# Weights of a feed-forward block loaded and decoded in 256-row chunks, with the masks built ahead of the branch

## The chip, the cores and the metric

The kernel runs on one core of a Trainium2 chip. The metric is the device time in microseconds (us); lower is better. TensorE (PE) multiplies matrices, VectorE (DVE) and ScalarE (ACT) work elementwise, GpSimd (POOL) fills small tiles, and SyncE (SP) issues the DMAs.

## What is computed

Three blocks stand one behind the other. The change touches what the first two need: the masks of the attention, and the weights `w_in` and `w_out` of the second block.

```python
# 1: banded attention, batch 2, 8 heads, 768 positions, head size 64
scores = q @ k.T / sqrt(64)
keep   = (pos_k < n_sink) | ((0 <= pos_q - pos_k) & (pos_q - pos_k < window))
a      = softmax(where(keep, scores, -1e9));   x = a @ v          # x: 2 x 768 x 512
# 2: gated feed-forward block
h      = relu(x @ w_in)                                           # w_in: 512 x 1024
gate   = sigmoid(conv3(h, conv_w));   x = (h * gate) @ w_out      # w_out: 1024 x 512
# 3: rotation by angles x @ w_theta, two token mixes (768 x 768), channel mix
z      = x * cos(x @ w_theta), x * sin(x @ w_theta)
u      = x + w_tok_r @ z_r + w_tok_i @ z_i;   out = u + relu(u @ w_ch)
```

`n_sink` (4) and `window` (128) are inputs, known only at run time. The weights arrive as 64-bit floats.

## The kernel before

**Order of the program.** `params` reads `n_sink` and `window` and works out a flag: do they allow the banded path, with at most two key blocks for a query block? Each engine loads that flag (`values_load`) and branches into `body`, in the banded form here. The instructions of `body` are put in order by a scheduler at build time; each engine then goes through its own list strictly in that order. SP too: a DMA whose tile isn't free yet holds up all DMAs behind it.

**Attention.** A *unit* is half the sequence of one batch element, four units in all. A unit has four pairs of heads, and each head has three *score tiles* of 128 queries (line 286 for the matmul, 288 for mask and maximum on DVE, 292 for the exponential on ACT). So there are 24 tiles in a unit and 96 in all; I count them as tile 1 to tile 96. The first tile of a batch element's first unit is 128 keys wide, others 260. Numbers 25 to 48 belong to the second unit. Behind the exponential comes the normalised probability, split in two halves, and its transpose: through PE for the first four heads (`transposed_by_pe`), through a DMA transpose (`pt<-pb`, line 322) for the others. `values` (line 190) makes the values ready for each pair of heads in the first unit of a batch element: load of `vt`, sum on ACT (203), scaled copy on ACT (209), subtraction on DVE (210), DMA transpose (`vp<-slot`, 212).

**Weights.** `weight_load` brings 128 rows by 512 columns of 64-bit words (512 KB) into a slot; `decode_parts` rebuilds 32-bit floats with one ACT operation (98) and three DVE operations (99, 100, 101), and `split` makes a high and a low part (80 on ACT, 82 on DVE): four DVE and two ACT operations of 512 elements for each of 16 chunks. The order is: four chunks for the first half of `w_in`, four for `w_out`, then the same again. The table `CHUNKS` says how many chunks are taken after which pair of heads of which unit. `BLOCKS` does the same for the feed-forward blocks (`Group.blocks`), whose matmuls are `ps_h` (122 to 124) and `ps_x` (616 to 622).

**Slots.** Weights and values share six slots of 4 KB on each partition, handed out in turn (`Slots`). A value takes two slots, one for the loaded rows, one for its two halves; a slot is free once its last reader is done.

**Ahead of the branch** stand the loads of chunk 0 and chunk 1, of the first queries and keys and of `conv_w`, the first three DVE steps of chunk 0 and the decoding of `conv_w`. The masks (`banded_masks`, lines 175 to 184) are built behind the branch.

Of the kernel before, what the change touches and what calls it, by code (L numbers as in the profile page):

```python
# [31 lines left out]
CHUNKS = ((1, 1, 3, 6), (2, 2, 0, 1), (0, 0, 0, 0), (0, 0, 0, 0))  # L32
# [4 lines left out]
DEC = 2  # L37
# [91 lines left out]
def params(tc, c, n_sink, window):  # L129

    nc = tc.nc
    raw = c.const.tile([P, 4], I32, name="par_raw")
    nc.sync.dma_start(raw[:, 0:2], n_sink.bitcast(I32).partition_broadcast(P))
    nc.sync.dma_start(raw[:, 2:4], window.bitcast(I32).partition_broadcast(P))
# [32 lines left out]
def banded_masks(tc, c):  # L167
# [3 lines left out]
    m, slot = c.raw.tile([P, 5 * P + 2 * NS], F32)  # L171
    m0, m1, m2 = m[:, :P], m[:, P : 3 * P + NS], m[:, 3 * P + NS :]
# [17 lines left out]
def values(tc, c, b, p):  # L190
# [533 lines left out]
def body(tc, c, general):  # L724
# [224 lines left out]
```

## Time and profile before

| what | us |
|---|---|
| median of 3 runs (461.37 to 462.35) | 461.46 |
| the profiled execution's own time | 463.23 |
| its span from first to last instruction | 461.4 |
| PE busy in the span | 413.2 |
| DVE busy in the span | 334.2 |
| ACT busy in the span | 291.5 |
| tile 1 starts on DVE | 14.87 |
| tile 48 (the second unit's last) starts on DVE | 108.31 |

Times in rows count from the start of the span. In a row of the timeline stand start, duration, engine, line, operation and, in brackets, how long the engine sat idle before it and what released it. In a row of the windows view stand, for each engine, busy time and number of instructions.

### The profile page before, as it was taken

Reading aid. Unit: us, or ns where it says so; the run is one execution under the profiler, and the core shown is the slowest. Engines: PE = TensorE matmul, PEld = TensorE weight load, DVE = VectorE, ACT = ScalarE, POOL = GpSimd, SP = SyncE. Lnnn points to the kernel's source line nnn. Section 1 sums busy time; section 2 is a strip of 40 time slices with the busy share of each in tenths; the row PEclk is TensorE's granted clock in tenths of the full one; section 3 lists DMA queues with packets and bytes.
Section 4 is the critical chain, followed back from the end, with each engine's and each line's share of the span. In section 5 each row is a group of like instructions: output and inputs, shape, how many; then the busy total and the mean of one; then the engine's idle time right before and its main releaser. Section 6 shows DMA issues by size and latency. Waiting matters only on the chain.

```text
span 461.4 us, 7204 instructions
## 1 busy us (share of the span) xinstructions
PE 413.2 (90%) x2376; PEld 334.9 (73%) x2376; DVE 334.2 (72%) x898; ACT 291.5 (63%) x717; POOL 35.5 (8%) x120
## 2 busy tenths in 40 slices
PE   1587739699889999999999999899979999999995
PEld 0465528587677887988888887688858888888874
DVE  3879989999889886865699877995599963211132
ACT  2799878978899886875685778875675431100010
POOL 4001210031221110110000000000000000000000
PEclk9989867899999999999999999999999999999999
DMA  6786999459888442212435200230037620000012
GB/s 180 208 230 148 248 247 293 107 117 201 181 169 166 103 92 48 47 38 39 139 88 164 70 1 0 70 92 23 0 93 223 195 84 23 24 23 24 23 45 75
DMA packets 73245, 50.07 MB, mean 109 GB/s; under 512 B 59376, under 2 KB 62448, under 8 KB 73200
## 3 DMA queue, kind: packets, MB, share of 16 engines
q1 hardware_dynamic: 73200, 49.54, 42.6%
q8 instruction: 20, 0.33, 0.3%
q14 instruction: 25, 0.20, 0.1%
HBM read 32.09 MB, written 3.15 MB: 76 GB/s over the span
## 4 chain that ended last, share of the span: by engine, by line
PE 67%; DVE 16%; DMA 8%; ACT 4%; issue 3%; SPq 1%; POOL 0%; DVEq 0%; ACTq 0%; POOLq 0%
PE ps_y L123 7%; PE ps_y L124 7%; PE ps_y L122 7%; PE ps_x L616 5%; PE ps_s L272 5%; PE ps_x L617 4%; PE ps_m L122 4%; PE ps_x L622 4%; PE ps_m L124 4%; PE ps_m L123 4%; PE ps_o L380 4%; PE ps_h L122 4%; PE ps_h L124 3%; PE ps_h L123 3%; DMA pt<-pb 3%
## 5 line engine op out<-in xcount | busy, mean ns | idle before, releaser
L272 PE MATMUL ps_s<-qk 128*128 128x260 f32 (+1 forms) x192 | 60.4, 420 | 20.4 <-DVE mx L288 11.1
L122 PE MATMUL ps_y<-z_hi,wt_hi 128*128 128x512 f32 x144 | 57.7, 401 | 1.6 <-ACT z_hi L80 1.6
L122 PE MATMUL ps_h<-xg_hi,win_hi 128*128 128x258 f32 x192 | 58.6, 307 | 0.4 <-ACT h L597 0.4
L124 PE MATMUL ps_y<-z_lo,wt_hi 128*128 128x512 f32 x144 | 56.7, 397 | 0.4 <-DVE z_lo L82 0.4
L123 PE MATMUL ps_y<-z_hi,wt_lo 128*128 128x512 f32 x144 | 56.9, 395 | 0.0
L124 PE MATMUL ps_h<-xg_lo,win_hi 128*128 128x258 f32 x192 | 56.0, 296 | 0.4 <-DVE xg_lo L401 0.3
L272 PEld LDWEIGHTS ps_s<-qk 128*128 128x128 f32 x192 | 34.2, 211 | 29.5 <-DVE mx L288 15.6
L123 PE MATMUL ps_h<-xg_hi,win_lo 128*128 128x258 f32 x192 | 55.4, 290 | 0.0
L80 ACT ACTIVATE xt_hi<-ps_t 128x512 fp32r<-128x512 f32 x24 | 14.0, 594 | 61.1 <-PE ps_t L650 61.0
L292 ACT ACTIVATE e<-e,mx 128x260 f32<-128x260 f32 (+1 forms) x96 | 47.3, 496 | 7.2 <-DVE mx L288 6.9
L601 DVE SCALAR_TENSOR_TENSOR cv<-h,cw_t,cv 128x256 f32<-128x256 f32 x96 | 44.8, 478 | 6.8 <-ACT cv L599 6.1
L288 DVE CUSTOM_DVE_ANT_0 e<-ps_s,m 128x260 f32<-128x260 f32 (+1 forms) x96 | 37.7, 399 | 10.4 <-PE ps_s L272 9.0
L616 PE MATMUL ps_x<-wout_hi,ghi 128*128 128x512 f32 x96 | 40.9, 426 | 3.4 <-ACT ghi L80 3.4
L718 DVE SCALAR_TENSOR_TENSOR slot<-ps_m,slot 128x512 f32<-128x512 f32 x12 | 8.3, 691 | 44.1 <-PE ps_m L124 44.1
L122 PEld LDWEIGHTS ps_h<-xg_hi,win_hi 128*128 128x128 f32 x192 | 36.8, 192 | 3.7 <-ACT h L597 1.2
L617 PE MATMUL ps_x<-wout_lo,ghi 128*128 128x512 f32 x96 | 38.7, 403 | 0.0
L124 PEld LDWEIGHTS ps_h<-xg_lo,win_hi 128*128 128x128 f32 x192 | 36.8, 193 | 1.9 <-issue 0.5
L123 PEld LDWEIGHTS ps_h<-xg_hi,win_lo 128*128 128x128 f32 x192 | 36.9, 192 | 1.4
L314 ACT ACTIVATE pb<-e,ri 128x256 f16<-128x256 f32 (+1 forms) x84 | 35.4, 494 | 1.9 <-DVE ri L296 1.2
L315 DVE SCALAR_TENSOR_TENSOR pb<-e,ri,pb 128x256 f16<-128x256 f32 (+1 forms) x84 | 35.5, 459 | 1.2 <-ACT pb L314 1.1
L380 PE MATMUL ps_o<-pt,vp 128*64 128x256 f16 (+2 forms) x348 | 23.8, 261 | 11.8 <-DMA pt<-pb 5.4
L380 PEld LDWEIGHTS <-vp 128*64 128x64 f16 (+1 forms) x348 | 17.9, 113 | 22.5 <-issue 13.3
(134 smaller groups left out, 927.6 us busy)
## 6 DMA issues: line engine op xcount, KB each, us to landing
raw<-in_w_tok_r_dram SPq DMA_DIRECT2D x12, 384.0 KB, 3.3
raw<-in_w_tok_i_dram SPq DMA_DIRECT2D x12, 384.0 KB, 3.5
slot<-in_w_in_dram SPq DMA_DIRECT2D x8, 512.0 KB, 6.1
slot<-in_w_out_dram SPq DMA_DIRECT2D x8, 512.0 KB, 4.7
qk<-in_q_dram SPq DMA_DIRECT2D x32, 96.0 KB, 3.3
slot<-in_vt_dram SPq DMA_DIRECT2D x8, 384.0 KB, 3.7
out_dram<-slot SPq DMA_DIRECT2D x12, 256.0 KB, 2.0
qk<-in_k_dram SPq DMA_DIRECT2D x8, 262.0 KB, 3.2
```

The lines of the kernel that those rows point to most:

```text
L122: nc.tensor.matmul(out, whi, xhi, start=first, stop=False)
L123: nc.tensor.matmul(out, wlo, xhi, start=False, stop=False)
L124: nc.tensor.matmul(out, whi, xlo, start=False, stop=last)
L272: nc.tensor.matmul(ps[:, :n], qk[0][:, a, i * P : (i + 1) * P], qk[1][:, o : o + n], start=True, stop=True)
L288: nc.vector.tensor_tensor_reduce(out=e[:, i, :n], in0=ps[:, :n], in1=m, scale=-1.0 / math.sqrt(D), scalar=3.0e38, op0=ALU.add, op1=ALU.min ...
L292: nc.scalar.activation(e[:, i, :n], e[:, i, :n], AF.Exp, bias=mx[:, i : i + 1], scale=-1.0, accum_out=sm[:, i : i + 1])
L314: nc.scalar.activation(hi, src, AF.Copy, scale=r)
L315: nc.vector.scalar_tensor_tensor(lo, src, r, hi, ALU.mult, ALU.subtract)
L380: nc.tensor.matmul(po[a * D : (a + 1) * D, q], w[:, a * D : (a + 1) * D], pts[a][: w.shape[0], b0:b1, :], start=(n == 0), stop=(n == len(j ...
L601: nc.vector.scalar_tensor_tensor(cv[:, n, :], h[:, n, k : GT + k], w[:, k : k + 1], cv[:, n, :], ALU.mult, ALU.add)
L616: nc.tensor.matmul(self.px[t], ghi[:, n, s], whi, start=f2 == 0 and n == 0, stop=False)
L617: nc.tensor.matmul(self.px[t], ghi[:, n, s], wlo, start=False, stop=False)
```

## The change

`params`: `window` is loaded through ACT's DMA queue, `n_sink` through SP's, and the flag comes after six DVE operations instead of ten. `banded_masks` is called ahead of the branch. The three decoding steps of chunk 0 and the decoding of `conv_w` are taken behind the branch. A weight chunk is 256 rows (1 MB), decoded in operations of 1024 elements: 8 chunks instead of 16, with `CHUNKS` rewritten. There are three slots of 8 KB instead of six of 4 KB. A value takes one slot: loaded rows in one half, its parts in the other. There is one buffer for `dec_t` (`DEC`) instead of two, of twice the size.

```diff
-CHUNKS = ((1, 1, 3, 6), (2, 2, 0, 1), (0, 0, 0, 0), (0, 0, 0, 0))
+CHUNKS = ((1, 0, 1, 3), (1, 1, 0, 1), (0, 0, 0, 0), (0, 0, 0, 0))
-DEC = 2
+DEC = 1
-EARLY = 1
@@ class Slots
-        self.free = [pool.tile([P, 2 * DM], I32, name=f"slot{i}") for i in range(n)]
+        self.free = [pool.tile([P, 4 * DM], I32, name=f"slot{i}") for i in range(n)]
@@ params
+    nc.scalar.dma_start(raw[:, 2:4], window.bitcast(I32).partition_broadcast(P))
     nc.sync.dma_start(raw[:, 0:2], n_sink.bitcast(I32).partition_broadcast(P))
-    nc.sync.dma_start(raw[:, 2:4], window.bitcast(I32).partition_broadcast(P))
...
-    nc.vector.tensor_copy(flag, t[:, 0:1])
+    nc.vector.scalar_tensor_tensor(flag, c.ns, float(NS), t[:, 1:2], ALU.is_le, ALU.mult)
+    w = c.const.tile([P, 2], F32, name="par_w")
+    nc.vector.scalar_tensor_tensor(w, flag.to_broadcast([P, 2]), 0.0, v, ALU.mult, ALU.add)
@@ values
-    raw, slot0 = c.raw.tile([P, S], F32)
+    both, slot = c.raw.pair(F32)
+    raw, parts = both[:, :S], both[:, S : 2 * S].bitcast(F16).rearrange("p (a k) -> p a k", a=2)
     nc.sync.dma_start(raw, c.vt[b, p * P : (p + 1) * P, :])
-    parts, slot1 = c.raw.tile([P, 2, S], F16)
@@ weight_load
-    n, i = divmod(i, 8)
-    if i < CC:
-        src = c.w_in[i * P : (i + 1) * P, 2 * n * DM : 2 * (n + 1) * DM]
+    n, i = divmod(i, 4)
+    if i < 2:
+        src = c.w_in[2 * i * P : 2 * (i + 1) * P, 2 * n * DM : 2 * (n + 1) * DM]
...
-    raw, slot = c.raw.tile([P, DM, 2], I32)
+    raw, slot = c.raw.pair()
@@ moe_weights
-        for tiles in (w1, w2):
-            for r in range(4):
...
+        for hi, lo in w1 + w2:
+            raw, slot = c.wraw.pop(0) if c.wraw else weight_load(tc, c, c.nw)
+            decode_parts(nc, c.dec, raw, hi, lo, INPLACE)
@@ body
-    if not general:
-        banded_masks(tc, c)
...
+        if n == 1:
+            conv_weights(tc, c)
@@ moe_stack
-        c.raw = Slots(c.const, B * NG)
+        c.raw = Slots(c.const, B * NG // 2)
...
-        with tc.tile_pool(name="dec0", bufs=1, side="right") as dec:
-            c.first = decode(nc, raw, dec.tile([P, DM], F32, name="dec_t"), True), slot
+        cw = conv_load(tc, c)
+        banded_masks(tc, c)
```

The engines' lists show where things stand now. First DVE, around the branch (`TENSOR_LOAD` and `COMPARE_AND_BRANCH`). Before:

```order
L150 CAST par_flag<-par_t 128x1
L99 TENSOR_SCALAR slot_100<-slot_100 128x512
L100 SCALAR_TENSOR_TENSOR slot_100<-dec_t,slot_100 128x512
L101 SCALAR_TENSOR_TENSOR slot_100<-slot_100 128x512
L99 TENSOR_SCALAR cw<-cw 128x24
L100 SCALAR_TENSOR_TENSOR cw_t<-cw_t,cw 128x24
L101 SCALAR_TENSOR_TENSOR cw_t<-cw,cw_t 128x24
L883 TENSOR_LOAD par_flag
L886 COMPARE_AND_BRANCH
L175 TENSOR_SCALAR slot_102<-rel 128x128
```

The same place now (the rows end with the first score tile and the first decoding step of the weights):

```order
L188 SCALAR_TENSOR_TENSOR slot_99<-col,par_w,slot_99 128x128
L191 TENSOR_SCALAR m_96<-slot_99 128x260
L191 TENSOR_SCALAR m_94<-slot_99 128x128
L191 TENSOR_SCALAR m_95<-slot_99 128x260
L888 TENSOR_LOAD par_flag
L892 COMPARE_AND_BRANCH
L295 ISA e,mx<-ps_s,m_94 128x128
L295 ISA mx 128x1
L106 TENSOR_SCALAR slot_98<-slot_98 128x1024
L106 TENSOR_SCALAR cw<-cw 128x24
```

The masks `m` moved ahead of the branch, and the decoding moved behind it, in between the score tiles.

Second SP, where the last two values of the first batch element and the first `w_out` chunks are brought in. Before, with six slots (numbers 100 to 105):

```order
L212 DMA_TRANSPOSE vp<-slot_104 128x12x128
L198 DMA slot_103<-in_vt_dram 128x768
L261 DMA qk_194<-in_q_dram 64x384
L212 DMA_TRANSPOSE vp<-slot_102 128x12x128
L551 DMA slot_105<-in_w_in_dram 128x1024
L261 DMA qk_194<-in_q_dram 64x384
L551 DMA slot_102<-in_w_out_dram 128x1024
L262 DMA qk_194<-in_k_dram 128x524
L261 DMA qk_197<-in_q_dram 64x384
L212 DMA_TRANSPOSE vp<-slot_104 128x12x128
```

Now, with three slots (98 to 100); ahead of these rows stand the first value's transpose from `slot_100` and the next load of `vt` into `slot_100`:

```order
L219 DMA_TRANSPOSE vp<-slot_99 128x12x128
L206 DMA slot_99<-in_vt_dram 128x768
L268 DMA qk_189<-in_q_dram 64x384 x2
L269 DMA qk_189<-in_k_dram 128x524
L268 DMA qk_102<-in_q_dram 64x384
L219 DMA_TRANSPOSE vp<-slot_100 128x12x128
L219 DMA_TRANSPOSE vp<-slot_99 128x12x128
L329 DMA_TRANSPOSE pt<-pb_192 128x11x128
L562 DMA slot_100<-in_w_out_dram 128x2x1024
L562 DMA slot_99<-in_w_in_dram 128x2x1024
L268 DMA qk_102<-in_q_dram 64x384
L562 DMA slot_98<-in_w_out_dram 128x2x1024
```

Both `vt` loads now follow a transpose out of the very slot that they fill, and the first two loads of weights behind the values follow the last transposes out of `slot_100` and `slot_99`; three chunks of 1 MB stand together.

Third ACT, where those chunks are decoded, in the second unit. Before:

```order
L314 ACTIVATE pb_202<-e,ri 128x256 x3
L80 ACTIVATE wout_hi<-slot_100 128x512
L98 ACTIVATE dec_t<-slot_102 128x512
L98 ACTIVATE dec_t<-slot_101 128x512
L80 ACTIVATE wout_hi<-slot_105 128x512
L292 ACTIVATE e,sm<-e,mx 128x260
L314 ACTIVATE pb_204<-e,ri 128x256 x3
L292 ACTIVATE e,sm<-e,mx 128x260 x2
```

Now:

```order
L105 ACTIVATE dec_t<-slot_100 128x1024
L299 ACTIVATE e,sm<-e,mx 128x260 x2
L246 ACTIVATE vs<-ps_o 36x384
L299 ACTIVATE e,sm<-e,mx 128x260 x3
L105 ACTIVATE dec_t<-slot_98 128x1024
L299 ACTIVATE e,sm<-e,mx 128x260 x2
L87 ACTIVATE wout_hi<-slot_100 128x1024
L321 ACTIVATE pb_194<-e,ri 128x256 x3
```

The first decoding step of the second `w_out` chunk (`slot_98`, the last of the three loads on SP's list) stands five exponentials behind that of the first.

## Rows read from the trace of the kernel before

**Rows 1.** Windows: busy us and (instructions) of PE, PEld, DVE, ACT, POOL; clock, DMA, GB/s.
```profile
12.00:44.00 32.00, 23.11 (x140) 17.26 (x141) 27.01 (x110) 27.51 (x85) 1.09 (x5) 0.95 0.76 198
44.00:65.00 21.00, 13.29 (x83) 9.12 (x82) 19.16 (x64) 16.86 (x48) 4.51 (x13) 0.81 0.97 231
65.00:108.00 43.00, 36.22 (x232) 29.39 (x232) 42.51 (x121) 36.94 (x98) 6.11 (x16) 0.82 0.75 183
108.00:200.00 92.00, 88.09 (x650) 72.38 (x649) 76.25 (x267) 80.34 (x234) 16.53 (x53) 1.00 0.58 118
200.00:461.00 261.00, 250.88 (x1271) 205.85 (x1269) 164.94 (x322) 126.65 (x250) 1.24 (x3) 1.00 0.23 69
```

**Rows 2.** Timeline of the start, up to tile 1.
```profile
3.37 0.58 SPq L262 DMA_DIRECT2D qk<-in_k_dram  x1
...
5.30 0.17 DVE L136 CAST par_f<-par_raw 128x4 f32<-128x4 int32 x1 [3.55 <-DMA par_raw<-in_window_dram]
...
6.73 0.15 DVE L150 CAST par_flag<-par_t 128x1 int32<-128x1 f32 x1
...
10.51 0.22 ACT L98 ACTIVATE cw_t<-cw 128x24 f32<-128x24 f32 x1 [2.37 <-DMA cw<-in_conv_w_dram]
...
11.99 0.23 DVE L175 TENSOR_SCALAR slot<-rel 128x128 f32<-128x128 f32 x1 [0.55 <-DVE cw_t L101]
...
14.87 0.42 DVE L288 CUSTOM_DVE_ANT_0 e<-ps_s,m 128x260 f32<-128x260 f32 x1
```

**Rows 3.** DMA views: issues, count, KB each, us to landing; issued at 3.37, 15.93, 20.54, 22.54, 52.74, 55.96.
```profile
qk<-in_k_dram SPq DMA_DIRECT2D x1, 196.0 KB, 5.2
...
slot<-in_w_in_dram SPq DMA_DIRECT2D x1, 512.0 KB, 4.0
...
vp<-slot SPq DMA_TRANSPOSE x1, 4.4
...
slot<-in_vt_dram SPq DMA_DIRECT2D x1, 384.0 KB, 3.9
...
pt<-pb SPq DMA_TRANSPOSE x1, 10.1
...
slot<-in_w_in_dram SPq DMA_DIRECT2D x2, 512.0 KB, 8.5
```

**Rows 4.** Windows of one us: loads of weights alone, then transposes.
```profile
53.00:54.00 1.00, 1.00 (x15) 0.91 (x16) 1.00 (x5) 0.00 (x0) 0.00 (x0) 0.70 1.00 393
...
59.00:60.00 1.00, 0.00 (x0) 0.00 (x0) 1.00 (x3) 1.00 (x5) 0.00 (x0) 1.00 2.35 100
```

**Rows 5.** Timeline: the stall in the second unit.
```profile
62.94 0.39 PE L380 MATMUL ps_o<-pt,vp 128*64 128x256 f16 x1 [4.94 <-DVE mx L288]
...
64.13 1.24 ACT L98 ACTIVATE dec_t<-slot 128x512 f32<-128x512 f32 x2 [2.55 <-DMA slot<-in_w_in_dram]
...
64.82 1.00 DVE L99 TENSOR_SCALAR slot<-slot 128x512 int32<-128x512 int32 x2 [1.32 <-ACT dec_t L98]
...
68.31 1.07 PE L380 MATMUL ps_o<-pt,vp 128*64 128x256 f16 x8 [2.95 <-DMA pt<-pb]
```

**Rows 6.** Groups by shape: count, busy us, mean ns of one, idle before.
```profile
L80 ACT ACTIVATE z_hi<-rkr 128x1024 fp32r<-128x1024 f32 x12 | 12.7, 1058 | 5.6 <-DVE rkr L682 5.5
...
L98 ACT ACTIVATE dec_t<-slot 128x512 f32<-128x512 f32 x16 | 10.6, 668 | 9.4 <-DMA slot<-in_w_in_dram 7.8 <-DMA slot<-in_w_out_dram 1.1 <-DVE cw L99 0.5
...
L99 DVE TENSOR_SCALAR slot<-slot 128x512 int32<-128x512 int32 x16 | 6.8, 424 | 3.3 <-ACT dec_t L98 3.2
```

**Rows 7.** Timeline of DVE in the third block: 512 and 1024 elements, back to back.
```profile
295.11 0.68 DVE L676 SCALAR_TENSOR_TENSOR rkr<-rkr,ps_m 128x512 f32<-128x512 f32 x1
295.70 1.22 DVE L82 TENSOR_TENSOR z_lo<-rkr,z_hi 128x1024 fp32r<-128x1024 f32 x1
296.84 0.55 DVE L82 TENSOR_TENSOR wt_lo<-dec_t,wt_hi 128x384 fp32r<-128x384 f32 x1
```

**Rows 8.** Timeline of DVE: tile 48, the second unit's last.
```profile
108.31 0.42 DVE L288 CUSTOM_DVE_ANT_0 e<-ps_s,m 128x260 f32<-128x260 f32 x1
```

More of the change, by code (lines that the diff above doesn't have):

```diff
@@ L69, in __init__, with pair, half @@
     def __init__(self, pool, n):
-        self.free = [pool.tile([P, 2 * DM], I32, name=f"slot{i}") for i in range(n)]
-    def tile(self, shape, dtype):
+        self.free = [pool.tile([P, 4 * DM], I32, name=f"slot{i}") for i in range(n)]
+        self.halves = []
+    def pair(self, dtype=I32):
         slot = self.free.pop(0)
-        t = slot.bitcast(dtype)[:, : math.prod(shape[1:])]
-        return (t if len(shape) == 2 else t.rearrange("p (a b) -> p a b", a=shape[1])), slot
+        return slot.bitcast(dtype), slot
+    def half(self, shape, dtype):
+        if not self.halves:
+            slot = self.free.pop(0)
+            self.halves = [slot[:, : 2 * DM], slot[:, 2 * DM :]]
+        t = self.halves.pop(0).bitcast(dtype)[:, : math.prod(shape[1:])]
+        return t if len(shape) == 2 else t.rearrange("p (a b) -> p a b", a=shape[1])
 def split(nc, hi, lo, src, scale=None):
@@ L170, in banded_masks @@
     rel, col = c.rel, c.col
-    m, slot = c.raw.tile([P, 5 * P + 2 * NS], F32)
-    m0, m1, m2 = m[:, :P], m[:, P : 3 * P + NS], m[:, 3 * P + NS :]
+    m, slot = c.raw.pair(F32)
+    m0, m1, m2 = m[:, :P], m[:, P : 3 * P + NS], m[:, 3 * P + NS : 5 * P + 2 * NS]
     cur = slice(KW, KW + P)
@@ L212, in values @@
     nc.sync.dma_start_transpose(out=v, in_=parts.rearrange("p a k -> p (a k)"))
-    c.raw.free += [slot0, slot1]
+    c.raw.free.append(slot)
     return v, unscale, sink_values(tc, c, v)
@@ L562, in moe_weights @@
         c.w2 += w2
-        for tiles in (w1, w2):
-            for r in range(4):
-                hi, lo = (x[:, r % 2, :] for x in tiles[r // 2])
-                if c.nw == 0:
-                    w, slot = c.first
-                    split(nc, hi, lo, w)
-                else:
-                    raw, slot = c.wraw.pop(0) if c.wraw else weight_load(tc, c, c.nw)
-                    decode_parts(nc, c.dec, raw, hi, lo, INPLACE)
-                c.nw += 1
-                c.raw.free.append(slot)
-                yield
+        for hi, lo in w1 + w2:
+            raw, slot = c.wraw.pop(0) if c.wraw else weight_load(tc, c, c.nw)
+            decode_parts(nc, c.dec, raw, hi, lo, INPLACE)
+            c.nw += 1
+            c.raw.free.append(slot)
+            yield
 class Group:
@@ L625, in blocks @@
         if f2 == FB // 2 - 1:
-            x2, _ = c.raw.tile([P, 2, DM], F32)
+            x2 = c.raw.half([P, 2, DM], F32)
             c.x2[b, 2 * g], c.x2[b, 2 * g + 1] = x2[:, 0, :], x2[:, 1, :]
@@ L779, in body @@
                 next(weights)
-                while len(c.wraw) < W_AHEAD[n] and c.nw + len(c.wraw) < 16:
+                while len(c.wraw) < W_AHEAD[n] and c.nw + len(c.wraw) < 8:
                     c.wraw.append(weight_load(tc, c, c.nw + len(c.wraw)))
```

33 lines of the change are left out of this document (16 added, 17 removed).

## The prediction

> **What bounds the kernel now.** I read the windows view first, cut where the work changes its kind [rows 1]. From 200 us on PE is busy in 250.88 of 261 us, and from 108 to 200 us in 88.09 of 92 us: there PE sets the time, with ACT close behind it (80.34). Nothing of the change lies there but the slots for finished rows, so a microsecond that the first two units win or lose goes to the end. Before 108 us PE idles a lot, and others set the time. From 65 to 108 us DVE is busy in 42.51 of 43 us. From 12 to 44 us ACT leads with 27.51 of 32 us, most of its idle time lying at the beginning. From 44 to 65 us stands a stall. The timeline shows its parts [rows 5]: ACT waits 2.55 us for weights until 64.13, DVE 1.32 us for ACT until 64.82, PE 4.94 us up to 62.94 and 2.95 us for a transpose up to 68.31. The DMA view says why: a DMA transpose took 10.1 us, and weights issued behind it 8.5 us, against 4.0 us for a load by itself [rows 3]. So the first question is when tile 48 comes, which stood at 108.31 [rows 8]. It hangs on the moment at which DVE resumes after the stall: 64.82, then 43.49 us of DVE work with next to no gap.
>
> **The start.** Before, DVE was done with the flag at 6.88 (6.73 + 0.15), sat in the decoding of `conv_w` (landed at 10.51), began the masks at 11.99 and tile 1 at 14.87 [rows 2]. Now the masks need only the flag. The window's load is on ACT's queue, which the trace doesn't show; I bound its landing from two sides: 5.3 us, where the cast began before, and 3.4 us, since a load of 512 KB by itself takes 4.0 us [rows 3], of which 1.3 us move data at 393 GB/s [rows 4], and 2.7 us are left for the smallest, issued at 0.7 us. The flag then comes after six operations instead of ten, some 1.0 us behind the cast instead of 1.6: between 4.4 and 6.3 us. A dozen mask operations of 0.2 to 0.35 us end by 7 to 9 us. That costs nothing, because queries and keys cover it: they now stand behind 1 MB instead of 512 KB. The bytes ahead of `conv_w` stay the same (chunk 0, chunk 1, queries and keys before; one chunk of twice the size and the same queries and keys now), so the keys land about when `conv_w` did, at 10.51, less one issue of 0.47 us on SP that is gone, and a little less for their place ahead of it: 9.9 us, instead of 8.6 (3.37 + 5.2, [rows 3]). Were that cover gone, the masks would cost at most their 2.6 us. Tile 1 starts half a microsecond of matmul later, at 10.4 instead of 14.87: **4.5 us ahead**.
>
> **Larger operations.** DVE goes from a 512-element operation to the next in 0.59 us (295.11 to 295.70) and from one of 1024 in 1.14 us (295.70 to 296.84) [rows 7]. A pair merged saves 0.04 to 0.06 us, some 1.5 to 1.9 us for 32 pairs; taken by whole durations (2 x 0.68 - 1.22) it would be 0.14 each, 4.5 us, the upper end. I take 1.9, since DVE's operations overlap. ACT: 2 x 668 - 1058 = 278 ns for each of 16 pairs [rows 6], 4.4 us as the upper end; it matters only where ACT leads. Against that, a score tile that stands behind such an operation waits up to 0.55 us more; in the first two chunks, while DVE still has gaps, eight operations could cost up to 4 us. I take 1 us: ACT must wait for the third decoding step before it can split chunk 0, with tile 5 behind that. The Trainium skill (Perfetto Trace Analysis, Optimizing Scalar/DVE Operations) advises larger operations where the engine is saturated and breaking them up where it isn't but holds up others. By its second half the merge would cost those 4 us at the start; by its first half it would gain in the 43 us after the stall; the rows show both conditions, one after the other.
>
> **Three slots.** This hands most of the start back. A value's transpose, next load, next transpose now follow one another in the same slot, and SP stands at each [rows 3]: 4.4 us to land a transpose, 3.9 us for the load. Between tile 1 (10.4) and the end of the first value's copy ACT has 6.9 us of work plus 2 us of waiting for DVE's long steps; DVE's subtraction (1 us) and SP's list put that transpose at 21.4, against 20.54. It lands at 25.8, the third value's load at 29.4; the second transpose goes out at 26.2, lands at 30.1, and the fourth value's load lands at 33.8. ACT gets there about 2 us earlier and waits. Then come its sum, seven small operations and the last two copies, ending near 39.5, a subtraction of 1 us on DVE, and the two last transposes, issued at 38.9 and 40.6 and landing at 42.8 to 44.5. So the first `w_out` chunk is issued at about 43.5 and the other two by 46, with two transposes still in the engines until about 47 (an estimate: 2 to 3 us each of the 4.4 us to landing). Before, these loads came from 38 us on, in smaller pieces.
>
> **The burst.** Three chunks are 3.15 MB. Weights alone move at 393 GB/s, while transposes hold the rate at 100 [rows 4]. On SP's list no transpose stands between the three, unlike before. At 393 GB/s they take 8.0 us from 47; with some 1.5 us to land (of the 2.7 us that a lone load takes without its data, about half), the last (`slot_98`) is there at **56.7**. If the transposes don't delay them, it is 54.5; at 231 GB/s, the mean of the old stall [rows 1], 13.6 us from 45 to 47 give 60 to 62. The list of ACT has the decoding of `slot_98` five exponentials behind that of `slot_100`, so ACT asks for it at about 55. The Trainium skill (Perfetto Trace Analysis, DMA Optimizations) has two rules here: larger transfers fill the memory's bandwidth better, and splitting may let some work start sooner. By the first nothing changes, as pieces of 512 KB already reach 393 GB/s here; by the second, halves would land 1.3 us sooner, which would put the forecast below at 458.3, and is what the change gives away.
>
> **What is left of DVE's work.** ACT's step of 1024 elements takes 1.06 us [rows 6], so DVE resumes at 57.8, against 64.82. But it has more to do until tile 48. In its list there stood 33 decoding steps of 512 elements after the resume (8 of line 99, 25 others); now there are 42, made as 21 of 1024: 5 x 0.61 + 16 x 1.14 = 21.3 us instead of 8 x 0.34 + 25 x 0.60 = 17.7. The 0.61 and 0.34 follow from the 424 ns for 512 elements [rows 6] less the overlap of 0.08 us. Three more halvings of probabilities and two more stores of `x`, one score tile less: 1.5 us. So 43.5 + 3.6 + 1.5 = 48.6 us, and tile 48 comes at 57.8 + 48.6 = 106.4: **1.9 us earlier**.
>
> **The tail.** After tile 48 the same matmuls, conversions and blocks are left, in nearly the same order, and the slots for finished rows are free long before. I count nothing for it, with 1 us to either side for the scheduler's order. ACT has a little more work up to tile 96, but PE leads.
>
> **Sum.** The profiled execution took 463.23 us, its span 461.4; 1.9 us less gives 461.3 for the execution and 459.5 for the span. The execution lay 0.4% above the median of the three runs, 461.46. The same 1.9 us against that median: **459.6 us**, 0.4% less.
>
> **Rivals.** *The start is kept.* If the transposes don't hold up the burst, `slot_98` is there before ACT asks at 55, DVE resumes at 56, and tile 48 comes at 104.6: 3.7 us earlier, 457.8; with another us from ACT's shorter steps, 456.8. For it speaks that no transpose stands between the loads, against it that three transposes go out in the 4 us ahead of them. *The start isn't there.* If queries and keys land 2 us later than I think, so do all the links of the chain, `slot_98` comes at 58.7, DVE resumes at 59.7 and tile 48 stands where it stood: 461.4. The change then doesn't do what the shorter flag suggests, since the flag was never last. *The slots cost more than the start gives.* One place decides: the landing of `slot_98`. From 58.7 on, each microsecond later makes the kernel a microsecond slower. Were the fourth value's load another 2 us late, or the burst at 231 GB/s, it would land at 61, and tile 48 at 110.7: 463.9. Speaking for it: the old trace shows loads of 512 KB taking 8.5 us behind transposes [rows 3]; against it: those stood behind two transposes that now come later on the list. The Trainium skill's advice on splitting (Perfetto Trace Analysis, DMA Optimizations) points to this side.
>
> **How the numbers follow.** Forecast, 459.6: 0.38. Start kept, 457.3: 0.18. Start not there, 461.4: 0.19. Slots cost more, 463.9: 0.25. Within 0.2%, 0.92 us, no measurement of this kernel tells a change from none; 460.5 and 462.4 are the bounds. The forecast's own spread of 1.5 us leaves a little of it within them, and some of the third case beyond them. That gives faster 0.54, same 0.20, slower 0.26. The range reaches over the first three cases and most of the fourth: 456.3 to 464.0. Faster cases hold most of the chance; for the likeliest alone I would say 458 to 461.
>
> **What would show it.** In the changed kernel's timeline: tile 1 at 10 to 11 us, right behind the keys' landing and with the masks done; ACT waiting at the fourth value's sum at 32 to 34 us; the three 1 MB loads issued from 43 to 46 us; ACT waiting for `slot_98` up to some 56.7 us; then DVE without gaps, tile 48 at 106 us, and from there 353 us as before. I am wrong if `slot_98` isn't the last thing waited for in the second unit, if DVE shows gaps after it, or if the stretch after tile 48 changes by more than 1 us.

## The result and the profile after

The changed kernel takes 466.02 us (median of 4 runs, 465.08 to 466.77), against 461.48 us before: a ratio of 1.0093, 95% interval 1.0070 to 1.0116. It is slower by 4.5 us where I had forecast 1.9 us less. The profiled execution took 466.32 us, its span 464.4. That is 3.0 us above the span before and not 4.5, because the kernel before was profiled in an execution 1.8 us above its median (463.23), the changed one in an execution 0.3 us above its own.

The windows view after, cut as in [rows 1], with the same columns:

```profile
12.00:44.00 32.00, 27.43 (x158) 19.66 (x157) 26.35 (x94) 28.46 (x85) 2.94 (x14) 0.89 0.61 168
44.00:65.00 21.00, 12.21 (x67) 8.35 (x67) 17.87 (x58) 16.90 (x46) 7.17 (x17) 0.88 1.07 270
65.00:108.00 43.00, 36.47 (x232) 29.27 (x230) 40.60 (x97) 34.69 (x81) 4.32 (x15) 0.86 0.67 172
108.00:200.00 92.00, 86.57 (x621) 71.83 (x621) 75.47 (x260) 77.66 (x227) 13.70 (x50) 0.96 0.65 128
200.00:464.00 264.00, 254.01 (x1301) 208.58 (x1299) 169.63 (x337) 130.99 (x263) 1.98 (x6) 1.00 0.22 68
```

Count matmuls, the numbers in brackets behind PE's busy time. From 12 to 108 us PE did 457 (158 + 67 + 232), before 455 (140 + 83 + 232): the better start had been given back by 65 us, and at 108 us PE stood where it had stood (shape by shape, too, the counts differ by one matmul). From 108 to 200 us it did 621 instead of 650, and the granted clock was 0.96 instead of 1.00. At 200 us it had 254.01 us of work in front of it instead of 250.88, and those 3.1 us are, to 0.1 us, the difference of the two spans (464.4 and 461.4).

The stretch in which PE lost its 29 matmuls begins at 108 us. Windows of 2 us:

```profile
108.00:110.00 2.00, 1.23 (x5) 0.67 (x4) 2.00 (x6) 1.22 (x5) 0.00 (x0) 1.00 0.72 221
110.00:112.00 2.00, 0.88 (x3) 0.82 (x4) 2.00 (x8) 0.96 (x4) 0.00 (x0) 0.83 1.36 185
112.00:114.00 2.00, 1.77 (x4) 0.66 (x4) 1.76 (x13) 1.96 (x7) 1.03 (x4) 0.50 0.73 131
114.00:116.00 2.00, 1.14 (x15) 1.14 (x16) 1.75 (x7) 2.00 (x7) 0.64 (x3) 0.50 1.12 236
116.00:118.00 2.00, 2.00 (x21) 1.66 (x18) 1.62 (x3) 1.83 (x6) 0.00 (x0) 0.50 0.77 237
```

From 108 to 112 us DVE is busy without a gap and PE for 2.11 of 4 us. Then PE's granted clock is 0.50 (the lower of its two levels, 1.2 GHz) until 118 us. The timeline names what PE waited for, first tile 48 on DVE, then PE:

```profile
111.06 0.41 DVE L295 CUSTOM_DVE_ANT_0 e<-ps_s,m 128x260 f32<-128x260 f32 x1
...
111.12 2.65 PE L279 MATMUL ps_s<-qk 128*128 128x128 f32 x6 [1.66 <-DVE mx L295]
114.86 1.54 PE L387 MATMUL ps_o<-pt,vp 128*64 128x128 f16 x15 [1.08 <-DMA pt<-pb]
```

Tile 48 came at 111.06 instead of 108.31 [rows 8], DVE being late, and PE's list held no block of the feed-forward between 109.5 and 118.3 us to fill the gap. From 110 to 124 us PE's idle time of 2.6 us and the lower clock, worth 2.7 us (an estimate: the sum of busy time times 1 minus the clock, in windows of 2 us), stand against 0.6 and 0 before.

**How the delay arose.** The start, to be read beside [rows 2]:

```profile
1.68 2.08 SPq L268 DMA_DIRECT2D qk<-in_q_dram  x2
3.80 1.09 SPq L269 DMA_DIRECT2D qk<-in_k_dram  x1
...
6.86 0.17 DVE L143 CAST par_f<-par_raw 128x4 f32<-128x4 int32 x1 [4.97 <-DMA par_raw<-in_n_sink_dram]
...
11.18 2.50 PE L279 MATMUL ps_s<-qk 128*128 128x128 f32 x6 [11.18 <-DMA qk<-in_k_dram]
12.09 0.29 DVE L295 CUSTOM_DVE_ANT_0 e<-ps_s,m 128x128 f32<-128x128 f32 x1 [1.98 <-PE ps_s L279]
```

Tile 1 waits for the keys, 2.8 us ahead of before. Then SP's queue, the slots' chain, to be read beside [rows 3]:

```profile
23.68 1.94 SPq L219 DMA_TRANSPOSE vp<-slot  x1
25.68 0.83 SPq L206 DMA_DIRECT2D slot<-in_vt_dram  x1
26.61 1.28 SPq L219 DMA_TRANSPOSE vp<-slot  x1
27.95 1.10 SPq L206 DMA_DIRECT2D slot<-in_vt_dram  x1
...
41.92 3.29 SPq L219 DMA_TRANSPOSE vp<-slot  x2
45.31 1.71 SPq L329 DMA_TRANSPOSE pt<-pb  x1
47.12 0.76 SPq L562 DMA_DIRECT2D slot<-in_w_out_dram  x1
47.97 0.42 SPq L562 DMA_DIRECT2D slot<-in_w_in_dram  x1
...
49.06 0.54 SPq L562 DMA_DIRECT2D slot<-in_w_out_dram  x1
...
50.21 11.53 SPq L329 DMA_TRANSPOSE pt<-pb  x3
...
66.34 8.26 SPq L329 DMA_TRANSPOSE pt<-pb  x3
74.70 0.94 SPq L562 DMA_DIRECT2D slot<-in_w_out_dram  x1
```

And the stall that answers to [rows 5], with the later wait for weights:

```profile
52.72 1.12 ACT L105 ACTIVATE dec_t<-slot 128x1024 f32<-128x1024 f32 x1 [1.13 <-DMA slot<-in_w_out_dram]
59.23 1.12 ACT L105 ACTIVATE dec_t<-slot 128x1024 f32<-128x1024 f32 x1 [2.53 <-DMA slot<-in_w_out_dram]
...
80.98 1.14 ACT L105 ACTIVATE dec_t<-slot 128x1024 f32<-128x1024 f32 x1 [3.27 <-DMA slot<-in_w_out_dram]
```

DVE resumes the decoding at 60.38 us instead of 64.82, but tile 48 is then 50.7 us away instead of 43.5.

### The profile page after: what moved, and what is told of

It reads as the page before. It is cut to its first block, busy times and chain, and to the rows that moved or that the text cites. A ratio compares the mean times of both kernels' runs of the same rounds, so it can differ in the third digit from the quotient of the medians.

```text
span 464.4 us, 7139 instructions
## 1 busy us (share of the span) xinstructions
PE 417.5 (90%) x2376; PEld 338.5 (73%) x2376; DVE 333.6 (72%) x863; ACT 291.4 (63%) x701; POOL 35.2 (8%) x120
## 3 DMA queue, kind: packets, MB, share of 16 engines
HBM read 32.09 MB, written 3.15 MB: 76 GB/s over the span
## 4 chain that ended last, share of the span: by engine, by line
PE 68%; DVE 14%; DMA 11%; ACT 3%; issue 3%; SPq 1%; POOL 0%; DVEq 0%; ACTq 0%; POOLq 0%
PE ps_y L131 7%; PE ps_y L130 7%; PE ps_y L129 7%; PE ps_s L279 5%; PE ps_x L621 4%; DMA pt<-pb 4%; PE ps_m L129 4%; PE ps_m L131 4%; PE ps_x L622 4%; PE ps_m L130 4%; PE ps_x L627 4%; PE ps_h L129 4%; PE ps_h L131 4%; PE ps_h L130 4%; PE ps_o L387 4%; DMA slot<-in_w_out_dram 4%
## 5 line engine op out<-in xcount | busy, mean ns | idle before, releaser
L279 PE MATMUL ps_s<-qk 128*128 128x260 f32 (+1 forms) x192 | 59.6, 425 | 21.4 <-DMA qk<-in_k_dram 11.2
L606 DVE SCALAR_TENSOR_TENSOR cv<-h,cw_t,cv 128x256 f32<-128x256 f32 x96 | 44.8, 480 | 7.3 <-ACT cv L604 6.7
L622 PE MATMUL ps_x<-wout_lo,ghi 128*128 128x512 f32 x96 | 38.9, 406 | 0.0
L129 PEld LDWEIGHTS ps_y<-z_hi,wt_hi 128*128 128x128 f32 x144 | 27.0, 188 | 8.0 <-ACT z_hi L87 2.1
L387 PE MATMUL ps_o<-pt,vp 128*64 128x256 f16 (+2 forms) x348 | 25.9, 273 | 7.0 <-DMA pt<-pb 6.9
```

The lines of the kernel that those rows point to most:

```text
L129: nc.tensor.matmul(out, whi, xhi, start=first, stop=False)
L279: nc.tensor.matmul(ps[:, :n], qk[0][:, a, i * P : (i + 1) * P], qk[1][:, o : o + n], start=True, stop=True)
L387: nc.tensor.matmul(po[a * D : (a + 1) * D, q], w[:, a * D : (a + 1) * D], pts[a][: w.shape[0], b0:b1, :], start=(n == 0), stop=(n == len(j ...
L606: nc.vector.scalar_tensor_tensor(cv[:, n, :], h[:, n, k : GT + k], w[:, k : k + 1], cv[:, n, :], ALU.mult, ALU.add)
L622: nc.tensor.matmul(self.px[t], ghi[:, n, s], wlo, start=False, stop=False)
```

## The experiments

A caution first: the instructions of `body` are put in order by a scheduler at build time, so every edit also changes the order of much of what follows. A run compares an edit together with the order that comes of it. "PE left" is the busy time of PE after 200 us in the windows view of the profiled execution: 250.88 us before, 254.01 after. After 200 us PE is busy for 95 to 97% of the time in every kernel, so this number says little more than the span of that one execution, and it can stand off the median: b_front_dec was profiled at 474.2 us, j1_ops_512_one_buffer at 461.1 (its slowest execution), c_chunks_ops_512 at 465.9, j1_half at 456.6. Ratios are to the kernel before, taken on the same chip. The chips differ from group to group, so small differences between kernels are better read from the ratios.

| kernel | us | ratio, 95% interval | PE left |
|---|---|---|---|
| changed kernel | 466.0 | 1.0093 (1.0070 to 1.0116) | 254.0 |
| a_front | 466.7 | 1.0103 (1.0077 to 1.0128) | 253.3 |
| b_front_dec | 471.9 | 1.0209 (1.0180 to 1.0239) | 260.1 |
| c_chunks | 470.1 | 1.0179 (1.0139 to 1.0218) | 259.0 |
| e_qk_first | 461.8 | 1.0006 (0.9983 to 1.0029) | 250.3 |
| f_half_front | 464.7 | 1.0062 (1.0039 to 1.0086) | 253.0 |
| k_swap | 466.0 | 1.0088 (1.0055 to 1.0122) | 253.5 |
| m_qk_first_third | 467.3 | 1.0129 (1.0099 to 1.0160) | 253.5 |
| l_half_swap | 464.4 | 1.0054 (1.0036 to 1.0072) | 253.1 |
| q_weights_pool | 472.7 | 1.0244 (1.0216 to 1.0273) | 257.5 |
| q_qk_first_pool | 468.4 | 1.0145 (1.0128 to 1.0162) | 253.5 |
| h_before_coarse | 464.2 | 1.0066 (1.0050 to 1.0082) | 253.4 |
| j_ops_512 | 460.9 | 0.9983 (0.9966 to 1.0001) | 248.0 |
| j1_ops_512_one_buffer | 457.3 | 0.9902 (0.9874 to 0.9930) | 250.5 |
| s_dve_512 | 463.0 | 1.0015 (0.9995 to 1.0034) | 251.2 |
| j_ops_512_half | 459.0 | 0.9935 (0.9911 to 0.9960) | 246.3 |
| j_qk_ops_512 | 464.5 | 1.0053 (1.0030 to 1.0076) | 252.6 |
| c_chunks_ops_512 | 462.3 | 1.0010 (0.9982 to 1.0038) | 252.3 |
| j1_half | 458.4 | 0.9946 (0.9919 to 0.9974) | 246.3 |

**Which part of the change costs.** Theory "slots": the three large slots delay the weights. Rival "front": the new start does. Three kernels hold parts of the change, a fourth takes the 1 MB load from ahead of the keys.

a_front is the kernel before with the new `params` and the masks ahead of the branch.

```diff
+    nc.scalar.dma_start(raw[:, 2:4], window.bitcast(I32).partition_broadcast(P))
...
-    if not general:
-        banded_masks(tc, c)
...
+        banded_masks(tc, c)
         c.slots = list(c.raw.free)
```

> The kernel before (128-row chunks, six slots of 4 KB) with one part of the change: the new parameters and the masks ahead of the branch; the decoding of chunk 0 and of conv_w stays ahead of it too. Theory 'slots' (the loss of the change comes from three large slots, so that 3 MB of weights can be issued only at 47 us): this part alone is a gain. DVE begins tile 1 about 2.9 us sooner (12.0 instead of 14.87), and most of it goes to the end: 458.5 to 460.0 us. Theory 'front' (the loss comes from the new start itself): no gain, 461.5 or more.

b_front_dec takes the decoding of chunk 0 and of `conv_w` behind the branch as well, in 128-row chunks.

```diff
+        if n == 1:
+            conv_weights(tc, c)
...
-            c.first = decode(nc, raw, dec.tile([P, DM], F32, name="dec_t"), True), slot
+        c.early = [(raw, slot)] + [weight_load(tc, c, n) for n in range(1, 1 + EARLY)]
```

> As the run before, and the decoding of chunk 0 and of conv_w moved behind the branch as in the change; still 128-row chunks and six slots. Theory 'slots': the keys now land behind 512 KB, at 8.6 to 9.5 us, tile 1 stands at 9.5 to 10.5 us, and 2.5 us of decoding come back between the tiles: 457.5 to 459.5 us. Theory 'front': decoding between the first tiles holds ACT up, 461.5 or more.

c_chunks is the changed kernel with the start of the kernel before (its `params`, masks behind the branch, first decoding ahead of it).

```diff
-        banded_masks(tc, c)
+        conv_weights(tc, c)
+            c.first = decode(nc, raw, dec.tile([P, 2 * DM], F32, name="dec_t"), True), slot
```

> The changed kernel with the start of the kernel before: old parameters, masks behind the branch, decoding of chunk 0 (now 256 rows) and conv_w ahead of it; chunks of 256 rows and three slots of 8 KB as in the change. Theory 'slots': the whole loss and none of the gain, 467 to 470 us, with the three loads of 1 MB issued at 48 us or later and ACT waiting for the last. Theory 'front': 461 to 463 us, since the new start is gone.

e_qk_first is the changed kernel with the first queries and keys loaded ahead of chunk 0.

```diff
-        raw, slot = weight_load(tc, c, 0)
         c.qk = [qk_buffer(nc, c.const, 0)]
         c.loaded = [load_qk(tc, c, 0)]
+        c.early = [weight_load(tc, c, 0)]
```

> The changed kernel with one line moved: the first queries and keys are issued ahead of the first weight chunk instead of behind it. In the changed kernel the keys landed at 11.05 us behind 1 MB, and tile 1 stood at 12.09. Now they land at 7 to 8 us and tile 1 stands at 9.5 to 10 us, once the masks are done. Theory 'slots': the chain of values and weights moves by at most 2 us, 464 to 466 us. Theory 'front' (1 MB ahead of the keys is what cost the time): 462 us or less.

Measured: 466.7, 471.9, 470.1 and 461.8 us. Neither theory holds. Each of the first three costs 5 to 10 us, and all parts together 4.5 us: the parts don't add. In a_front tile 1 even comes 1.65 us earlier than before (13.22), and with no large operation in the kernel it is still 1% slower; in its trace PE stands 5.3 us, from 44 to 65 us, for the transpose of a value. Whether that wait is the cause was not tested. Loading the keys first gives back 4.2 us, but its SP list differs in one more thing: it loads the second `w_out` chunk ahead of the next `w_in` chunk.

**Start, or order of the loads?** Four kernels take the two apart. f_half_front loads chunk 0 in two halves around the queries and keys; k_swap gives the second `w_out` chunk the slot that comes free first, so that it is loaded second; m_qk_first_third is e_qk_first with the order of loads turned back, by the same two lines; l_half_swap has halves and swap.

```diff
 # f_half_front
-        raw, slot = weight_load(tc, c, 0)
+        raw, slot = c.raw.pair()
+        rows = raw.rearrange("p (r n) -> p r n", r=2)
+        nc.sync.dma_start(rows[:, 0, :], c.w_in[0:P, 0 : 2 * DM])
         c.qk = [qk_buffer(nc, c.const, 0)]
         c.loaded = [load_qk(tc, c, 0)]
+        nc.sync.dma_start(rows[:, 1, :], c.w_in[P : 2 * P, 0 : 2 * DM])
 # k_swap, m_qk_first_third: in weight_load
+    if i == 3:
+        c.raw.free.insert(0, c.raw.free.pop(1))
```

> The changed kernel, but chunk 0 is loaded by two DMAs of 512 KB as in the kernel before: the first half ahead of the first queries and keys, the second behind them. The order of the three later weight loads on SP stays that of the changed kernel (w_out, w_in, w_out). Theory 'front' (the 1 MB load ahead of the keys shifts the start and with it the burst of weight loads; this is what loading the keys first gave back): tile 1 at 10 to 10.5 instead of 12.1, the decoding after the stall resumes near 58.5 instead of 60.4, time 462 to 463.5. Theory 'order' (what the kernel with the keys first gained came from its second w_out chunk being loaded ahead of the w_in chunk): tile 1 earlier all the same, but the resume at 60 to 60.5 and the time 465 to 466.5.

> The changed kernel, but the second w_out chunk takes the slot that comes free first, and the w_in chunk the one that comes free last, so that SP issues w_out, w_out, w_in instead of w_out, w_in, w_out. The start is untouched (tile 1 at 12.1). Theory 'order': the second w_out chunk, issued at 48.0 instead of 49.1 and landing in the 8.2 us of the load that stood there, is in at 56.2 instead of 59.2; decoding resumes near 57.4, 3 us earlier, time 463 to 464. Theory 'front': the swap is worth at most 1 us, time 465 to 466.

> The kernel with the keys ahead of the first weight chunk, but with the order of loads that the changed kernel has (w_out, w_in, w_out). Theory 'front': it keeps its gain, 461.5 to 463. Theory 'order': it loses it, 464.5 to 466. If both add, 463 to 464.5.

> Both edits on the changed kernel: chunk 0 in two halves around the first queries and keys, and the second w_out chunk loaded ahead of the w_in chunk. Theory 'front': as with the halves alone, 462 to 463.5. Theory 'order': as with the swap alone, 463 to 464. If both add: tile 1 at 10 to 10.5, decoding resumes at 55.5 to 56.5, time 459 to 461.

Measured: 464.7, 466.0, 467.3 and 464.4 us. The halves move tile 1 to 10.32 us and give 1.3 us, a third of what e_qk_first gave; the intervals of their ratios overlap, so those 1.3 us are not clear of noise. The swap does to its load what it should: ACT begins the second `w_out` chunk 3.3 us earlier and without a wait. In k_swap's timeline of ACT:

```profile
55.96 1.11 ACT L105 ACTIVATE dec_t<-slot 128x1024 f32<-128x1024 f32 x1
```

Yet tile 48 comes at 109.97, and the kernel takes the same time as the changed one. So the landing of that chunk, on which my prediction hung, doesn't decide. Nor does tile 48: in m_qk_first_third it comes at 105.46, 5.6 us ahead of the changed kernel, which is no slower. With the keys first, the order of the loads was worth 5.4 us (467.3 against 461.8); with the keys late, nothing. Both theories fall as single causes.

**SP's queue, the coarse order, the size of the operations.** q_weights_pool issues the chunks after the first from GpSimd's queue, past the DMA transposes on which SP stands; q_qk_first_pool does so in e_qk_first. h_before_coarse is the kernel before with the coarse order alone. j_ops_512 is the changed kernel with each 256-row chunk decoded in two lots of 512 elements and two buffers of `dec_t` of half the size.

```diff
 # q_weights_pool, q_qk_first_pool
+    queue = tc.nc.gpsimd if i else tc.nc.sync
...
-    tc.nc.sync.dma_start(raw.rearrange("p (r n) -> p r n", r=2), ...
+    queue.dma_start(raw.rearrange("p (r n) -> p r n", r=2), ...
 # h_before_coarse, on the kernel before
-CHUNKS = ((1, 1, 3, 6), (2, 2, 0, 1), (0, 0, 0, 0), (0, 0, 0, 0))
+CHUNKS = ((2, 0, 2, 6), (2, 2, 0, 2), (0, 0, 0, 0), (0, 0, 0, 0))
 # j_ops_512
-DEC = 1
+DEC = 2
...
-            decode_parts(nc, c.dec, raw, hi, lo, INPLACE)
+            for r in range(2):
+                decode_parts(nc, c.dec, raw[:, r * DM : (r + 1) * DM], hi[:, r, :], lo[:, r, :], INPLACE)
```

> The changed kernel, but the weight chunks after the first are issued by GpSimd's queue instead of SP's. Theory 'queue' (what is lost between the stall and tile 48 comes from SP: the last w_out chunks and the values' loads of the second batch element stand behind pt transposes, the last but one chunk from 66.3 to 74.7; DVE then has 2.4 us of gaps from 90 to 100, PE starves from 108 to 112 and runs at half clock from 112 to 118): no ACT wait on that chunk near 81, DVE without gaps from 90 to 100, PE busy for over 4.5 of the 5 us from 110 to 115 at clock 1.0, tile 48 near 108, time 462 to 464. Theory 'slots' (three slots are the limit, whoever issues): the loads start no earlier than a slot is free, the waits stay, time 465 to 467.

> The same on the kernel that loads the first queries and keys ahead of the first weight chunk (461.8). Theory 'queue': its own starved stretch at 98 to 102 goes as well, 459 to 460.5. Theory 'slots': 461 to 463.

> The kernel before with its six 4-KB slots and 128-row chunks, but taken in the coarse order of the changed kernel (its CHUNKS doubled: 2,0,2,6 and 2,2,0,2). Theory 'order': the coarse order is what made the large chunks alone lose 8.2 us, so 467 to 471. Theory 'slots': the order alone costs little, 461 to 464, and the loss came from three large slots.

> The changed kernel, but every 256-row chunk is decoded in two lots of operations of 512 elements (two buffers of dec_t of half the size). If the larger operations save the 1.9 us of DVE that the prediction put to them: 467 to 468.5. If that time lies beside a wait anyway: 465.5 to 466.5. If smaller pieces let the score tiles in between, so that DVE is less late at tile 48: 463 to 465.

Measured: 472.7, 468.4, 464.2 and 460.9 us. The queue theory falls: GpSimd holds its own small steps of the probabilities (`sk`, `pb`) behind the weights, and in q_weights_pool ACT waited 5.84 us for a transpose (that this is the whole loss isn't shown). The coarse order costs 2.4 us by itself. The small operations, which in the best of my three cases were to give 1 to 3 us, give 5.2 us.

DVE does have more to do with them. Groups by shape from 8 to 112 us (count, busy us, mean ns of one), the changed kernel:

```profile
L107 DVE SCALAR_TENSOR_TENSOR slot<-dec_t,slot 128x1024 int32<-128x1024 int32 x8 | 9.8, 1219 | 0.0
L106 DVE TENSOR_SCALAR slot<-slot 128x1024 int32<-128x1024 int32 x8 | 6.0, 756 | 2.6 <-ACT dec_t L105 2.6
```

and j_ops_512:

```profile
L107 DVE SCALAR_TENSOR_TENSOR slot<-dec_t,slot 128x512 int32<-128x512 int32 x16 | 10.9, 682 | 0.0
L106 DVE TENSOR_SCALAR slot<-slot 128x512 int32<-128x512 int32 x16 | 6.7, 417 | 0.8 <-ACT dec_t L105 0.8
```

What falls in one stretch is PE's waiting. How long PE waited for a score tile on DVE from 44 to 65 us (total, times, longest), the changed kernel, then j_ops_512, then j1_ops_512_one_buffer, which follows below:

```profile
PE ps_s L279 <- DVE mx L295: 5.2, 5, 1.6
```

```profile
PE ps_s L279 <- DVE mx L295: 1.9, 4, 1.0
```

```profile
PE ps_s L279 <- DVE mx L295: 0.3, 1, 0.3
```

In that stretch PE did 109 matmuls in j_ops_512 instead of 67. The same wait is 3.1 to 5.3 us in all eight kernels that have the changed kernel's masks ahead of the branch, large chunks and large operations, and 0 to 2.3 us in the six of them with DVE's steps in 512.

But this wait can't be the whole cause. The kernel before, all in operations of 512, waited longer for DVE in the same stretch, 7.5 us:

```profile
PE ps_o L380 <- DVE mx L288: 4.9, 1, 4.9
PE ps_s L272 <- DVE mx L288: 2.6, 2, 1.8
```

a_front has none of it and is 1% slower. Nor do the fast kernels gain in one place. From 12 to 108 us PE did 457 matmuls in the changed kernel, 494 in j_ops_512 and 465 in j1_ops_512_one_buffer; from 108 to 200 us 621, 612 and 633. So j_ops_512 gains ahead of the starved stretch, and keeps that stretch (clock 0.50 from 110 to 116 us); the other, in its slowest execution, does 8 more ahead of 108 us and 12 more behind it. Two of j_ops_512's windows:

```profile
44.00:65.00 21.00, 16.60 (x109) 11.44 (x107) 17.53 (x60) 19.50 (x58) 3.82 (x13) 0.91 1.13 273
108.00:200.00 92.00, 87.63 (x612) 73.27 (x613) 76.96 (x264) 81.31 (x235) 14.03 (x50) 0.96 0.59 119
```

And a rival came along with the small operations: SP's list is another one. In the eight kernels (in two of them on GpSimd's queue) the three loads of 1 MB go out within 2 to 3 us, the first at 44.5 to 47.7 us. In the six with small steps the first goes out at 42.8 to 44.8, and DMA transposes stand between the three, which take 7.6 to 11.9 us to go out. In j1_ops_512_one_buffer:

```profile
44.77 0.38 SPq L562 DMA_DIRECT2D slot<-in_w_out_dram  x1
45.25 2.41 SPq L219 DMA_TRANSPOSE vp<-slot  x1
47.76 6.57 SPq L329 DMA_TRANSPOSE pt<-pb  x3
54.39 1.58 SPq L562 DMA_DIRECT2D slot<-in_w_out_dram  x1
56.01 0.47 SPq L562 DMA_DIRECT2D slot<-in_w_in_dram  x1
```

No run held this order fixed. Against it as the only cause stand c_chunks and c_chunks_ops_512 (below): the three loads go out within 3 to 5 us in both, and the small operations gain all the same.

**Pieces, buffers, or a lucky order?** j1_ops_512_one_buffer has one buffer of `dec_t` (`DEC = 1`). s_dve_512 halves DVE's steps alone, ACT's stay at 1024. j_ops_512_half and j_qk_ops_512 put the small operations on f_half_front and e_qk_first. c_chunks_ops_512 puts them on c_chunks (one buffer; the first decoding ahead of the branch stays in 1024), and j1_half on f_half_front with one buffer. The edit is that of j_ops_512; in s_dve_512 the loop over the two halves stands around DVE's four steps only:

```diff
+    nc.scalar.activation(t, words[:, :, 1].bitcast(F32), AF.Copy, scale=2.0**-112)
+    for r in range(2):
+        part = words[:, r * DM : (r + 1) * DM]
...
+        nc.vector.tensor_scalar(high, high, -(2**31), None, ALU.bitwise_and)
```

> As the kernel with decoding in operations of 512 elements (460.85), but with one buffer of dec_t instead of two. Theory 'pieces' (an operation of 1024 elements holds up the score tiles queued behind it on DVE and ACT; halves let them in): keeps the gain, 460 to 462. Theory 'buffers' (the gain came from ACT running one decoding step ahead of DVE): 464 to 467. Theory 'order' (the gain belongs to the one order of instructions that the scheduler came to): no forecast better than 459 to 470.

> The changed kernel with only the DVE steps of the decoding in operations of 512 elements; ACT's two steps stay at 1024 with one buffer of dec_t. DVE then pays 4.5 us for the smaller operations, ACT nothing. Theory 'pieces', if DVE's queue is what matters: 460 to 463. If ACT's pieces or its second buffer matter: 465.5 to 468.

> Decoding in operations of 512 elements, and chunk 0 loaded in two halves around the first queries and keys; the order of the later DMAs on SP is the same as with the small operations alone. If the earlier start (1.3 us on the changed kernel) comes through: 459 to 460.2. If another wait takes its place: 460.5 to 461.5.

> Decoding in operations of 512 elements, and the first queries and keys loaded ahead of the first weight chunk. If both gains add (4.2 and 5.2 us on the changed kernel): 456 to 458. If both came out of the same stall: 460 to 462.

> The kernel with the old start and the large chunks (256-row loads, three 8-KB slots, 470.1), but decoding behind the branch in operations of 512 elements with one buffer of dec_t. Theory 'pieces': the large operations were what made it slow, 460 to 464. Theory 'order or slots': it stays at 467 to 471.

> Decoding in operations of 512 elements with one buffer of dec_t, and chunk 0 loaded in two halves around the first queries and keys. If the earlier start adds (1.3 to 1.8 us in the two runs that had it): 455 to 456.5. If another wait takes its place: 457 to 459.

Measured: 457.3, 463.0, 459.0, 464.5, 462.3 and 458.4 us. The second buffer isn't needed; with one the kernel is faster still, while on f_half_front one buffer and two can't be told apart (0.9946 and 0.9935). DVE's halves alone give 3.0 of the 5.2 to 8.7 us. In the four kernels in which I could compare, small against large operations give 5.2 or 8.7 us (changed kernel, two buffers or one), 5.7 or 6.3 (f_half_front) and 7.8 (c_chunks), but with the keys first they cost 2.7. (By the ratios, since the chips differ: 5.1 or 8.8, 5.9 or 5.4, 7.8, and a cost of 2.2.) There tile 1, which had come at 8.60, comes at 11.38, behind a decoding step that waits 2.26 us for ACT. In the timeline of DVE of j_qk_ops_512:

```profile
10.61 0.85 DVE L106 TENSOR_SCALAR slot<-slot 128x512 int32<-128x512 int32 x1 [2.26 <-ACT dec_t L105]
11.38 0.27 DVE L295 CUSTOM_DVE_ANT_0 e<-ps_s,m 128x128 f32<-128x128 f32 x1
```

That this late start is what costs the 2.7 us isn't shown. So small pieces are faster in three of four settings and slower in the fourth. In c_chunks PE's wait for score tiles from 44 to 65 us was small already (1.2 us) and with the small operations it was 2.9, so its 7.8 us came by another way that I did not follow up.

The pieces also get the first half of a chunk through earlier. In the changed kernel ACT begins the first `w_out` chunk at 52.72, and DVE ends its last step at 63.85:

```profile
62.66 1.19 DVE L89 TENSOR_TENSOR wout_lo<-slot,wout_hi 128x1024 fp32r<-128x1024 f32 x1
```

In j1_ops_512_one_buffer it begins at 50.39, and the halves are done at 58.15 and 61.03, 7.8 and 10.6 us later instead of 11.1:

```profile
50.39 0.66 ACT L105 ACTIVATE dec_t<-slot 128x512 f32<-128x512 f32 x1 [0.88 <-DMA slot<-in_w_out_dram]
...
57.47 0.68 DVE L89 TENSOR_TENSOR wout_lo<-slot,wout_hi 128x512 fp32r<-128x512 f32 x1
60.35 0.68 DVE L89 TENSOR_TENSOR wout_lo<-slot,wout_hi 128x512 fp32r<-128x512 f32 x1
```

j1_ops_512_one_buffer beats both kernels: 0.9902 of the kernel before (0.9874 to 0.9930), and 0.981 of the changed one (0.9902 / 1.0093). It keeps everything of the change but the 1024-element operations. Its interval overlaps with those of j1_half and j_ops_512_half, so which of the three is best stays open.

## Why the prediction was wrong, step by step

**The start: partly right.** The masks are hidden, as I said. But the keys landed at 11.18 instead of 9.9, and tile 1 gained 2.8 us instead of 4.5. I had moved the keys' issue earlier by one issue (0.47 us). In fact the two issues of queries took 2.08 us with 1 MB in front of them, against 1.19 before, so the keys were issued at 3.80, later than before. In f_half_front, with that load halved, tile 1 came at 10.32. The Trainium skill's remark (Perfetto Trace Analysis, DMA Optimizations) that splitting a transfer may let some work start sooner agrees with this, 1.8 us earlier than in the changed kernel.

**Larger operations: the step that failed.** The gain on DVE was sized well: by the distance between starts of neighbouring rows, 0.605 us for line 106 and 1.13 to 1.14 for the other three against twice 0.335 and 0.604, a chunk saves some 0.29 us, eight chunks 2.3 us (I said 1.9; 32 pairs at my 0.04 us were 1.3 and not 1.5). The price was not. I allowed 1 us for score tiles that wait behind large operations, and at the start only. Undoing this one edit made the kernel 5.2 us faster, or 8.7 with one buffer, with the same slots and masks and the same loads, though in another order on SP's list. My two conditions of the Trainium skill (Perfetto Trace Analysis, Optimizing Scalar/DVE Operations: larger operations on a saturated engine, smaller ones where an unsaturated engine holds up others) ask the right question, and j_ops_512 agrees with the second by its time. I applied it to the first two chunks only. From 44 to 65 us DVE is busy 17.87 of 21 us, and PE stands 5.2 us waiting for its score tiles. That is less than the 7.5 us before, so the size of the price is shown by the times, and where it is paid is not.

**Three slots: direction right, too short.** The first value's transpose went out at 23.68 instead of 21.4, the last two at 41.92 instead of 38.9 and 40.6, the weights from 47.12 instead of 43.5. The wait that I placed at the fourth value's load didn't come.

**The burst: right place, wrong importance.** The three loads took 12.1 us from first issue to last landing (47.12 to 59.23): 260 GB/s for 3.15 MB, where I had taken 393 and, for the rival, 231. (My 47 + 8.0 + 1.5 is 56.5 and not the 56.7 that I carried on.) But by k_swap, having the second `w_out` chunk 3.3 us earlier changes nothing in the time. The rival "The slots cost more than the start gives" came near in time (463.9) and had the sign, with the same wrong hinge.

**DVE without gaps: wrong.** From 65 to 108 us DVE idled 2.4 us (40.60 of 43), where before it idled 0.49, and tile 48 came 50.7 us after the resume instead of 48.6. Two things on my own list of what would prove me wrong happened: gaps on DVE, and a later wait for weights (80.98, 3.27 us), whose load stood behind three transposes on SP.

**The tail: right by its number, by luck.** From tile 48 to the end it took 353.3 us, as I said. But PE's own place at 108 us was that of before, and its loss came from 108 to 124 us (73 matmuls instead of 116), partly by the lower clock, which my sum didn't have at all. Nor is that stretch a constant, as my sum had it: over the twenty kernels profiled here it lies between 351.5 us (e_qk_first) and 367.3 us (j1_ops_512_one_buffer). So a microsecond won at tile 48 is not a microsecond won at the end.

**The sum.** By spans the forecast was 459.5 us and the measurement 464.4: 2.6 us of the difference lie ahead of the resume (60.38 instead of 57.8), 2.1 between the resume and tile 48, 0.2 behind it. The medians lie 6.4 us apart (466.0 and 459.6); the other 1.5 us come from which executions were profiled.

What stays open is how much of the operations' effect is the waiting itself and how much the other order, on the engines and on SP, that the scheduler makes of smaller pieces: no run kept the order and changed the size alone. Why the new start alone costs 1% (a_front) stays open too.

## What to carry over

Merging operations saves overhead on their engine (here some 2.3 us) and can cost more elsewhere (here 5.2 to 8.7 us): before you merge, ask which engines wait for what stands behind the merged operations, not only how busy their engine is. Where a scheduler orders the work, measure the parts of a change both alone and together, because here they didn't add. And count what the last bound engine has done at a few fixed times (here PE's matmuls at 108 and at 200 us): that told apart stretches where a single milestone, tile 48, misled.

## What the hardware did that I had not expected

The two parameter loads of 1 KB took 6.0 and 5.8 us to land when a 1 MB load was issued 0.45 us behind them, against 2.6 and 4.0 us before; with the queries and keys behind them instead (e_qk_first) 4.1 and 4.0. The size of the load behind them is only part of it: in a_front, with 512 KB behind them at the same distance, they took 5.4 and 4.3. The DMA view of the changed kernel's first 13 us (count, KB, us to landing):

```profile
slot<-in_w_in_dram SPq DMA_DIRECT2D x1, 1024.0 KB, 9.0
...
par_raw<-in_window_dram ACTq DMA_DIRECT2D x1, 1.0 KB, 5.8
par_raw<-in_n_sink_dram SPq DMA_DIRECT2D x1, 1.0 KB, 6.0
```

So here a small load wasn't safe from the one behind it, though it was issued first, and the one on ACT's queue no more than the one on SP's. And the starved PE paid twice: behind 4 us in which it was busy for 2.11, its clock fell to 0.50 and stayed there until 118 us, through 2 us in which it was busy without a gap.
